# Blocks of 512 and 480 tokens, another form of 1+elu, and six of eight chunk pairs split whole

## The chip, the cores and the metric

The kernel runs on one core of a Trainium2 chip. The metric is the device time of one execution in microseconds. The engines are called PE (TensorE, matrix products; PEld is its weight load), DVE (VectorE), ACT (ScalarE), POOL (GpSimd) and SP (SyncE, which issues the transfers). Each works through its own instructions in order and waits at semaphores for the others. Matrix products write to PSUM, eight banks of 512 float32 values per partition; everything else lies in SBUF.

## The reference

Two stages, cut to what matters:

```
# x: 4 batches of 12480 tokens of 128 channels; inducing: 32 rows
def mab(q, kv):
    s = scale * (q @ kv.T);  a = softmax(s);  return a @ kv
h = mab(inducing, x)              # 32 rows per batch
y = mab(x, h)                     # 4 x 12480 rows of 128
g = elu(y @ w_in)                 # 49920 x 2048
out = g @ w_out                   # 49920 x 128
```

The kernel folds `h @ w_in` into one matrix `hw` of 32 rows per batch, so that layer one of the feed-forward is softmax(x h^T) times `hw`.

## The kernel before

**Blocks and pairs.** The tokens of a batch come in 26 blocks of T = 480, all four batches in 104 blocks. For each block the 2048 hidden channels are sixteen chunks of 128, taken as eight pairs (`cp` 0 to 7). A unit `n` is one pair of one block; there are 832. Tokens are the columns throughout: a pair is a tile of 128 partitions and 2 x 480 columns.

**One unit.** `ffn_in` (L518) does layer one: two matmuls (L523) of a chunk of `hw` against the block's `stk` tile, which holds the softmax weights of the block as stacked high and low parts, in the format fp32r. Result: `ph`, two banks of PSUM; the pool `ps_h` has three such tiles. ACT then writes `e` = exp(ph) (L531). `ffn_mid` (L534) makes elu: for seven of eight pairs ACT clamps the exponential with a Relu (L538) and DVE takes the maximum with `ph` (L539); for the pair with the letter D in `CLAMP` DVE does both (L543, L546). With that `ph` is free. `ffn_split` (L548) copies the first of the two chunks to fp32r as `gh` (DVE, L552; in fp32r a part of 12 bits is exact), and POOL makes the rest `gl` (L555). `ffn_out` (L557) is layer two (L575): the chunk that isn't split goes as one float32 matmul (`e` against `wo_n`), the split one as three fp32r matmuls (`gh` against `wo_h` and `wo_l`, `gl` against `wo_h`). They accumulate in `po`, one bank; after the eighth pair DVE transposes it (L582) and SP stores it.

**Order.** PE runs in the written order: layer one of unit n, then layer two of unit n - LAG, with LAG = 6. The other engines get their order from a planner ahead of time. `e` lies in EB = 7 buffers, `gh` and `gl` in GB = 4 each; a buffer that is still to be read makes the writer wait.

**Attention.** For a batch's first stage and for the softmax of the second, groups of four blocks are worked on beside the feed-forward: scores by PE (L273, L449), exponentials by ACT, transposes and sums by DVE, the subtraction and the normalising by POOL (L466, L479), gathering by PE (L347). `attend_stack` (L483) splits the weights into `ahi` and `alo`; SP copies them into the `stk` tiles, four pieces of 32 rows for a block. `stack_h` builds `hw` in the same way. `attend` and `first_half` hold the places of these steps, counted in blocks, in tables. The last batch has no such work beside its later blocks.

**Start.** `first_batch` loads batch 0 and the weights, which come as float64 pairs of words and are taken apart by `Weight` on DVE, ACT and POOL; then the feed-forward begins. The first block goes alone.

```
for n, (b, k, cp) in enumerate(units):
    ffn_in(n)
    while done <= n - min(LAG, RAMP + n // 4):
        ffn_out(done)
        done += 1
    if n >= 1:
        ffn_mid(n - 1)
        ffn_split(n - 1)
    while side and side[0][0] <= n / NCP:
        side.pop(0)[1]()
```

Of the kernel before, what the change touches and what calls it, by code (L numbers as in the profile page):

```python
# [17 lines left out]
P = 128  # L18
Q = 32
T = 480  # L20
U = T // Q
# [9 lines left out]
def kernel(  # L31
# [12 lines left out]
    assert C == P and M == Q and N % T == 0 and F % 256 == 0  # L44
    NBLK = N // T
    GROUPS = [(g, min(4, NBLK - g)) for g in range(0, NBLK, 4)]
    NG = len(GROUPS)
    NH = (NBLK + 1) // 2
# [3 lines left out]
    assert len(SPLIT) == NCP  # L52
    CHUNKS_S = [2 * cp + i for cp in range(NCP) for i in range(SPLIT[cp] + MORE[cp])]
    CHUNKS_N = [f for f in range(NFC) if f % 2 >= SPLIT[f // 2]]
# [16 lines left out]
    xtp = ctx.enter_context(tc.tile_pool(name="xtp", bufs=NH + 2))  # L71
# [15 lines left out]
    # Two banks of PSUM take turns for a block's output; the one at rest serves the attention.  # L87
# [33 lines left out]
    # The feed-forward's weights come as float64: sign, 11 bits of exponent, 52 of mantissa. They  # L121
    # are read as pairs of 32-bit words and rounded to float32 here.
# [10 lines left out]
    class Weight:  # L133
        """A slice of float64 weights on its way to float32."""

        def __init__(self, raw):
            self.raw = raw.rearrange("p (f two) -> p f two", two=2)

        def take_apart(self):
            lo, hi = self.raw[:, :, 0], self.raw[:, :, 1]  # L140
            part = [
                stk.tile([P, WS], U32, tag="stk", name=f"w_{n}")
                for n in ("exp", "scale", "low", "top")
            ]
            e, scale, low, top = part
            nc.vector.tensor_scalar(
                out=e, in0=hi, scalar1=20, scalar2=0x7FF,
                op0=ALU.logical_shift_right, op1=ALU.bitwise_and,
            )
            nc.scalar.activation(e.bitcast(F32), e, AF.Relu, bias=rebias)  # L150
            nc.scalar.activation(
                e.bitcast(F32), e.bitcast(F32), AF.Relu, bias=largest, scale=-1.0
            )
            nc.gpsimd.tensor_scalar(
                out=scale, in0=e.bitcast(F32), scalar1=-254.0, scalar2=-float(1 << 23),
                op0=ALU.add, op1=ALU.mult,
            )
            nc.vector.tensor_scalar(
                out=top, in0=hi, scalar1=0xFFFFF, scalar2=0x100000,
                op0=ALU.bitwise_and, op1=ALU.bitwise_or,  # L160
            )
            nc.scalar.activation(low.bitcast(F32), lo, AF.Copy, scale=2.0**-52)
            nc.scalar.activation(e.bitcast(F32), hi.bitcast(I32), AF.Sign)
            self.scale, self.low, self.top = scale.bitcast(F32), low.bitcast(F32), top
            self.sign = e.bitcast(F32)
# [50 lines left out]
    def load_xT(b, h):  # L216
        n = min(2, NBLK - 2 * h) * T
        xq = xqp.tile([P, 2 * U, Q], F32, tag="xq", name=f"xq_{b}_{h}")
        src = x[b, 2 * h * T : 2 * h * T + n, :]
        for dq in range(4):  # L220
            nc.sync.dma_start(
                xq[dq * Q : (dq + 1) * Q, : n // Q, :],
                src[:, dq * Q : (dq + 1) * Q].rearrange("(u t) d -> t u d", t=Q),
            )
        t = xtp.tile([P, 2 * T], F32, tag="xT", name=f"xT_{b}_{h}")
        tc.keep_in_program_order(
            nc.vector.transpose(t[:, :n], xq.rearrange("p u d -> p (u d)")[:, :n])  # L227
        )
        xT[b, h] = t

    def transpose_first(b, g):
        """x^T of a group out of its tokens on the partitions."""
        g0, nq = GROUPS[g]
        np_ = nq * Q
        halves = []
        for h in range(g0 // 2, (g0 + nq + 1) // 2):
            xT[b, h] = xtp.tile([P, 2 * T], F32, tag="xT", name=f"xT_{b}_{h}")
            halves.append(xT[b, h].rearrange("p (j t u) -> p j t u", j=2, u=U))
        for v in range(0, U, UP):
            n = min(UP, U - v)  # L240
# [26 lines left out]
    def scores(b, g):  # L267
        g0, nq = GROUPS[g]
# [11 lines left out]
        # Within a block, token t * U + u goes to column (u, t).  # L280
# [10 lines left out]
    # The softmax over the tokens goes in two phases of groups: the first takes the maximum of its  # L291
    # own groups, the second that of all, and scales what the first has summed.
# [48 lines left out]
    def gather(b, g):  # L341
        st = state[b]
        np_ = GROUPS[g][1] * Q
# [74 lines left out]
    def stack_h(b):  # L418
        # Rows: high, low, high, low; against them the rows of a are high, high, low, low.
# [3 lines left out]
        for c in range(4):  # L423
            for i in range(4):
# [3 lines left out]
                )  # L428
        st["hw"] = hw

# [1 line left out]
    # The very first block goes alone, its rows four times from the start.  # L432
    stacks = {}

    def blocks_of(b, g):
        g0, nq = GROUPS[max(g, 0)]
# [34 lines left out]
    def attend_norm(b, g):  # L471
        s = state[b]["s2", g]
        np_ = s.shape[0]
# [9 lines left out]
    def attend_stack(b, g):  # L483
        s = state[b]["s2", g].rearrange("p u m -> p (u m)")
        np_ = s.shape[0]
        aT = once.tile([P, T], F32, tag="aT", name=f"aT_{b}_{g}")[:np_]
        nc.vector.transpose(aT, s)  # L487
        if lone(b, g):
            t = op.tile([P, T], F32R, tag="o", name=f"stk_{b}_{g}")
            nc.scalar.copy(t, aT)  # L490
            low = t[2 * Q :]
            nc.vector.tensor_sub(low, aT[2 * Q :], low.bitcast(F32))
            stacks[b, 0] = t
# [267 lines left out]
```

## Time and profile before

| | |
|---|---|
| median of 3 runs | 1813.05 us (1812.02 to 1813.22) |
| profiled execution: span from the first to the last instruction | 1811.1 us; no other time of this execution is given |
| busy share of the span | PE 95%, DVE 92%, ACT 87%, POOL 66% |
| mean granted clock of TensorE | 0.992 |
| instructions | 25049 |

How to read the rows. A row of the groups has the line, the engine, the operation, the tile written and those read, the shapes and the count; behind the first bar the busy time in us and the mean of one in ns; behind the second bar the engine's idle time just before, and what ended most of it. A row of the timeline has the start, the duration, the engine and line, the tiles, and in brackets the idle time before it with what ended it; `x2` means several merged instructions. A row of the waits has the engine and line that waited, the one it waited for, the total in us, the times and the longest. A row of the windows has the stretch, its length, busy time and count of the instructions asked for, the granted clock and the DMA share and rate. A matmul's recorded end is modelled, and consecutive ones overlap in the records; distances between starts are surer. A plain float32 matmul shows as two records.

### The profile page before, as it was taken

How to read it: one execution, taken by the hardware profiler on the slowest of the kernel's cores; microseconds unless marked ns; L12 is line 12 of the kernel's file. 1: busy time of each engine (PE TensorE's matmuls, PEld its weight loads, DVE VectorE, ACT ScalarE, POOL GpSimd, SP SyncE). 2: the span in 40 equal slices, each digit the busy share in tenths (PEclk: the TensorE clock that was granted, in tenths of full speed). 3: DMA queues.
4: the chain of work that ended last, by engine and by line, in shares of the span. 5: the costliest groups of instructions: out<-in, count | busy, mean ns of one | idle time of the engine just before them, and what ended most of it. 6: DMA issues, size and time to landing. Idle time of an engine off the chain costs nothing.

```text
span 1811.1 us, 25049 instructions
## 1 busy us (share of the span) xinstructions
PE 1728.0 (95%) x7268; PEld 1139.2 (63%) x7268; DVE 1669.4 (92%) x2308; ACT 1570.9 (87%) x1804; POOL 1196.6 (66%) x1007
## 2 busy tenths in 40 slices
PE   7699999999999999999999999999999999999998
PEld 5356666666666666666665666666666666666665
DVE  6999899998899988999899999899899999999998
ACT  6888888889888888889898888888888988888886
POOL 3866666666766666666666666666667667777776
PEclk9799999999999999999999999999999999999999
DMA  6555232222245423222225343222122211111111
GB/s 236 113 85 93 47 72 61 52 51 48 58 69 93 74 55 72 39 60 45 53 53 94 57 80 66 45 55 44 22 54 42 39 33 23 35 31 22 28 16 18
DMA packets 391574, 105.67 MB, mean 58 GB/s; under 512 B 367216, under 2 KB 382480, under 8 KB 391184
## 3 DMA queue, kind: packets, MB, share of 16 engines
q1 hardware_dynamic: 391440, 104.08, 29.5%
q8 instruction: 60, 0.98, 0.2%
q14 instruction: 74, 0.61, 0.1%
HBM read 48.94 MB, written 25.56 MB: 41 GB/s over the span
## 4 chain that ended last, share of the span: by engine, by line
PE 76%; DVE 15%; issue 5%; ACT 2%; DMA 1%; POOL 1%; SPq 0%; DVEq 0%; ACTq 0%; POOLq 0%
PE po L575 53%; PE ph L523 18%; DVE e L539 4%; DVE gh L552 4%; DVE e L546 2%; PE ps_hh L347 1%; DVE xT L227 1%; PE ps_s L273 1%; PE ps_t L449 1%; ACT e L531 1%; DVE e L543 1%; DMA xq<-in_x_dram 1%; ACT e L538 1%; PE ps_x L244 1%; DVE aT L487 0%
## 5 line engine op out<-in xcount | busy, mean ns | idle before, releaser
L555 POOL TENSOR_TENSOR gl<-e,gh 128x480 fp32r<-128x480 f32 x850 | 1064.4, 1254 | 537.5 <-DVE gh L552 359.7
L531 ACT ACTIVATE e<-ph 128x960 f32<-128x960 f32 x832 | 798.6, 961 | 173.1 <-PE ph L523 151.3
L539 DVE SCALAR_TENSOR_TENSOR e<-e,ph 128x960 f32<-128x960 f32 x728 | 827.1, 1139 | 67.9 <-ACT e L538 63.6
L575 PE MATMUL po<-e,wo_n 128*128 128x480 f32 x1628 | 789.0, 566 | 0.2 <-DVE s L457 0.2
L538 ACT ACTIVATE e<-e 128x960 f32<-128x960 f32 x728 | 729.5, 1005 | 20.1
L575 PE MATMUL po<-gh,wo_h 128*128 128x480 f32 x850 | 629.8, 741 | 0.0
L523 PE MATMUL ph<-stk,hw 128*128 128x480 f32 x1648 | 508.9, 390 | 48.8 <-DVE e L546 25.4
L552 DVE CAST gh<-e 128x480 fp32r<-128x480 f32 x850 | 490.8, 579 | 35.0 <-issue 21.1
L523 PEld LDWEIGHTS ph<-stk,hw 128*128 128x128 f32 x1648 | 294.9, 188 | 169.8 <-PE po L575 67.4
L575 PEld LDWEIGHTS po<-e,wo_n 128*128 128x128 f32 x1628 | 306.8, 189 | 48.9 <-PE ph L523 0.6
L575 PE MATMUL po<-gh,wo_l 128*128 128x480 f32 x850 | 322.1, 379 | 0.0
L575 PE MATMUL po<-gl,wo_h 128*128 128x480 f32 x850 | 320.4, 380 | 0.0
L575 PEld LDWEIGHTS po<-gh,wo_l 128*128 128x128 f32 x850 | 161.0, 189 | 175.1 <-issue 174.1
L575 PEld LDWEIGHTS po<-gh,wo_h 128*128 128x128 f32 x850 | 160.4, 189 | 175.8 <-issue 174.1
L575 PEld LDWEIGHTS po<-gl,wo_h 128*128 128x128 f32 x850 | 159.7, 188 | 26.9 <-POOL gl L555 0.6
L546 DVE TENSOR_TENSOR e<-e,ph 128x960 f32<-128x960 f32 x104 | 118.7, 1141 | 0.9
L543 DVE TENSOR_SCALAR e<-e 128x960 f32<-128x960 f32 x104 | 72.9, 701 | 5.4 <-ACT e L531 5.4
L582 DVE STREAM_TRANSPOSE o<-po 128x480 f32<-128x480 f32 x104 | 69.6, 669 | 3.7 <-PE po L575 3.7
L466 POOL TENSOR_TENSOR s<-s,mx 128x480 f32<-128x480 f32 (+2 forms) x28 | 29.6, 1056 | 28.2 <-DVE mx L465 28.2
L227 DVE STREAM_TRANSPOSE xT<-xq 128x960 f32<-128x960 f32 x39 | 45.3, 1162 | 0.0
L498 POOL TENSOR_TENSOR alo<-aT,ahi 128x480 fp32r<-128x480 f32 (+2 forms) x28 | 36.2, 1293 | 6.0 <-ACT ahi L497 5.7
L347 PE MATMUL ps_hh<-xm,e 128*32 128x128 f32 (+1 forms) x840 | 32.4, 291 | 3.6 <-DVE h L356 1.2
(93 smaller groups left out, 530.1 us busy)
## 6 DMA issues: line engine op xcount, KB each, us to landing
out_dram<-o SPq DMA_DIRECT2D x416, 60.0 KB, 1.9
xq<-in_x_dram SPq DMA_DIRECT2D x156, 120.0 KB, 3.6
stk<-ahi SPq DMA_DIRECT2D x206, 60.0 KB, 2.0
stk<-alo SPq DMA_DIRECT2D x206, 60.0 KB, 2.0
xm<-in_x_dram SPq DMA_DIRECT2D x24, 512.0 KB, 4.5
xm<-in_x_dram SPq DMA_DIRECT2D x24, 448.0 KB, 3.7
w_raw<-in_moe_w_in_dram SPq DMA_DIRECT2D x2, 1024.0 KB, 9.0
w_raw<-in_moe_w_out_dram SPq DMA_DIRECT2D x4, 512.0 KB, 4.9
```

The lines of the kernel that those rows point to most:

```text
L227: nc.vector.transpose(t[:, :n], xq.rearrange("p u d -> p (u d)")[:, :n])
L347: nc.tensor.matmul(ps[c * Q : (c + 1) * Q, :C], st["e", g][:np_, u * Q : (u + 1) * Q], st["xm", g, u - u % UP][:np_, u % UP, :], start=(u ...
L523: nc.tensor.matmul(ph[:, i, :T], state[b]["hw"][:, f * P : (f + 1) * P], stacks[b, k], start=True, stop=True,)
L531: nc.scalar.activation(e, ph[:, :, :T], AF.Exp)
L538: nc.scalar.activation(e, e, AF.Relu, bias=1.0, scale=-1.0)
L539: nc.vector.scalar_tensor_tensor(out=e, in0=e, scalar=-1.0, in1=ph[:, :, :T], op0=ALU.mult, op1=ALU.max)
L543: nc.vector.tensor_scalar(out=e, in0=e, scalar1=1.0, scalar2=-1.0, op0=ALU.min, op1=ALU.add)
L546: nc.vector.tensor_tensor(out=e, in0=e, in1=ph[:, :, :T], op=ALU.max)
L552: nc.vector.tensor_copy(gh[i], e[:, i, :])
L555: nc.gpsimd.tensor_sub(gl[i], e[:, i, :], gh[i].bitcast(F32))
L575: nc.tensor.matmul(po[:, :T], w, g, start=(cp == 0 and i == 0), stop=(cp == NCP - 1 and i == len(parts) - 1),)
L582: nc.vector.transpose(o.rearrange("p u d -> p (u d)"), po[:, :T])
```

## The change

Tokens: a batch is now 25 blocks, 15 of 512 and 10 of 480, in seven groups (`GROUPING`), so 100 blocks and 800 units. Elu: a row of ones in `hw` against a constant row block of 1/32 in `stk` makes layer one give H = 1 + h, and the tile is then g = 1 + elu = min(exp(H - 1), max(H, 1)): ACT writes exp with a bias of -1, one DVE instruction does the rest for every pair. The pieces in `stk` and `hw` become three of 32 rows and a constant fourth.

Splitting: each pair has a letter. P (places 0, 3, 5): both chunks are split; ACT writes `gh` = g - 1 to fp32r, POOL takes 1 off `e` in place and subtracts `gh`. D (places 1, 4, 7): both chunks are split; DVE writes g over `ph` in PSUM, ACT writes `gh` from there, and DVE makes `gl` = (g - 1) - gh from `ph`. N (places 2, 6): neither is split; POOL takes 1 off `e`, and layer two has two float32 matmuls. In the last batch from block 8 on, place 6 is a D. `gh` and `gl` are now tiles of the whole pair.

Buffers: `e` has 5 (was 7), `gh` 4 and `gl` 3 (of double width), `stk` six fixed tiles (was 8), `xm` 2 (was 3), LAG is 5 (was 6). `ph` stays at 3. `first_batch` puts the tokens of batch 0 into the buffers of `xm`, `e`, `gh` and `gl`, and the weights are taken apart in place.

```diff
-T = 480
-SPLIT = [1, 1, 1, 1, 1, 1, 1, 1]
-MORE = [0, 0, 1, 0, 0, 0, 0, 0]
-CLAMP = "AAADAAAA"
+TM = 512
+GROUPING = [(4, 512), (4, 512), (4, 512), (3, 512), (4, 480), (4, 480), (2, 480)]
+PLAN = "PDNPDPND"
+PLAN_CALM = "PDNPDPDD"
...
-    LAG = 6
+    LAG = 5
-    EB = 7
-    GB = 4
+    EB = 5
+    GHB = 4
+    GLB = 3
-    XB = 3
+    XB = 2
+    STK = 6
...
     def stack_h(b):
         for c in range(4):
-            for i in range(4):
+            for i in range(3):
                 nc.sync.dma_start(
...
+        nc.gpsimd.memset(hw[3 * Q :, :].bitcast(F32), 1.0)
...
+    homes = []
+    for i in range(STK):
+        homes.append(stk.tile([P, TM], F32R, tag=f"stk{i}", name=f"stk{i}"))
+        nc.gpsimd.memset(homes[i][3 * Q :, :].bitcast(F32), 1.0 / Q)
+
+    def home(b, k):
+        T = BLOCKS[k][1]
+        stacks[b, k] = homes[(b * NBLK + k) % STK][:, :T]
+        return stacks[b, k]
...
         for j, k in enumerate(blocks_of(b, g)):
-            t = stk.tile([P, T], F32R, tag="stk", name=f"stk_{b}_{k}")
-            for c in range(4):
+            t = home(b, k)
+            for c in range(3):
...
         e = gp.tile([P, 2, T], F32, tag="e", name=f"e_{n}")
-        nc.scalar.activation(e, ph[:, :, :T], AF.Exp)
+        nc.scalar.activation(e, ph, AF.Exp, bias=-1.0)
...
     def ffn_mid(n):
-        if CLAMP[cp] == "A":
-            nc.scalar.activation(e, e, AF.Relu, bias=1.0, scale=-1.0)
-            nc.vector.scalar_tensor_tensor(
-                out=e, in0=e, scalar=-1.0, in1=ph[:, :, :T], op0=ALU.mult, op1=ALU.max
-            )
-        else:
-            ...
+        v = live[n]
+        v["g"] = v["ph"] if plan(n) == "D" else v["e"]
+        nc.vector.scalar_tensor_tensor(
+            out=v["g"], in0=v["ph"], scalar=1.0, in1=v["e"], op0=ALU.max, op1=ALU.min
+        )
+
     def ffn_split(n):
-        for i in range(split(n)):
-            gh.append(ghp.tile([P, T], F32R, tag="gh", name=f"gh_{n}_{i}"))
-            nc.vector.tensor_copy(gh[i], e[:, i, :])
-        for i in range(split(n)):
-            gl.append(glp.tile([P, T], F32R, tag="gl", name=f"gl_{n}_{i}"))
-            nc.gpsimd.tensor_sub(gl[i], e[:, i, :], gh[i].bitcast(F32))
+        v, how = live[n], plan(n)
+        shape = list(v["e"].shape)
+        if how != "N":
+            v["gh"] = ghp.tile(shape, F32R, tag="gh", name=f"gh_{n}")
+            nc.scalar.activation(v["gh"], v["g"], AF.Copy, bias=-1.0)
+        if how == "D":
+            v["gl"] = glp.tile(shape, F32R, tag="gl", name=f"gl_{n}")
+            nc.vector.scalar_tensor_tensor(
+                out=v["gl"], in0=v["g"], scalar=-1.0, in1=v["gh"].bitcast(F32),
+                op0=ALU.add, op1=ALU.subtract,
+            )
+        else:
+            nc.gpsimd.tensor_scalar(
+                out=v["e"], in0=v["e"], scalar1=-1.0, scalar2=1.0, op0=ALU.add, op1=ALU.mult
+            )
+        if how == "P":
+            v["gl"] = glp.tile(shape, F32R, tag="gl", name=f"gl_{n}")
+            nc.gpsimd.tensor_sub(v["gl"], v["e"], v["gh"].bitcast(F32))
...
     def attend(b, g):
-        first = {0: (0.0, 0.13), 1: (1.39, 0.35), 2: (2.3, 0.7)}
-        later = {0: (-2.58, 0.19), 1: (0.07, 0.38)}
-        at, gap = (later if b else first).get(g, (4 * g - 6.7, 0.92))
+        first = {0: (0.0, 0.13), 1: (1.39, 0.35)}
+        later = {0: (-2.58, 0.19), 1: (0.9, 0.38)}
+        at, gap = (later if b else first).get(g, (GROUPS[max(g, 0)][0] - 4.7, 0.92))
...
-        room = [(xmp, "xm")] * XB + [(gp, "e")] * EB
-        spare = [(xqp, "xq")] * 2 + [(xtp, "xT")] * 2
+        room = [(xmp, "xm")] * XB + [(gp, "e")] * EB + [(ghp, "gh")] * GHB + [(glp, "gl")] * GLB
```

More of the change, by code (lines that the diff above doesn't have):

```diff
@@ L43 @@
     F = w_in.shape[1] // 2
-    assert C == P and M == Q and N % T == 0 and F % 256 == 0
-    NBLK = N // T
-    GROUPS = [(g, min(4, NBLK - g)) for g in range(0, NBLK, 4)]
+    assert C == P and M == Q and F % 256 == 0
+    assert N == sum(n * t for n, t in GROUPING)
+    GROUPS, BLOCKS, HALVES = [], [], []
+    for n, t in GROUPING:
+        GROUPS.append((len(BLOCKS), n, t))
+        for j in range(0, n, 2):
+            HALVES.append((len(BLOCKS) + j, min(2, n - j), len(GROUPS) - 1))
+        for _ in range(n):
+            BLOCKS.append((sum(u for _, u in BLOCKS), t))
+    NBLK = len(BLOCKS)
     NG = len(GROUPS)
-    NH = (NBLK + 1) // 2
+    NH = len(HALVES)
+    HALF_OF = {k: (h, k - k0) for h, (k0, n, _) in enumerate(HALVES) for k in range(k0, k0 + n)}
     UP = 8
@@ L488, in attend_stack @@
         if lone(b, g):
[L489 to L493, printed above, removed]
+            t = home(b, 0)
+            nc.scalar.copy(t[: 3 * Q], aT[: 3 * Q])
+            low = t[2 * Q : 3 * Q]
+            nc.vector.tensor_sub(low, aT[2 * Q : 3 * Q], low.bitcast(F32))
             return
@@ L506, in attend_stack, with plan @@
                 )
-            stacks[b, k] = t
     outs = {}
     live = {}
-    def split(n):
+    def plan(n):
         b, k, cp = units[n]
-        return SPLIT[cp] + (MORE[cp] if b == B - 1 and k >= CALM else 0)
+        return (PLAN_CALM if b == B - 1 and k >= CALM else PLAN)[cp]
     def ffn_in(n):
         b, k, cp = units[n]
-        ph = ps_h.tile([P, 2, 512], F32, tag="ph", name=f"ph_{n}")
+        T = BLOCKS[k][1]
+        ph = ps_h.tile([P, 2, 512], F32, tag="ph", name=f"ph_{n}")[:, :, :T]
         for i in range(2):
@@ L565, in ffn_out @@
             f = 2 * cp + i
-            if i >= split(n):
-                parts.append((0, wo_n[:, WHERE_N[f], :], e[:, i, :]))
+            if how == "N":
+                parts.append((0, wo_n[:, WHERE_N[f], :], v["e"][:, i]))
             else:
                 w = WHERE_S[f]
-                parts.append((1, wo_h[:, w, :], gh[i]))
-                parts.append((1, wo_l[:, w, :], gh[i]))
-                parts.append((2, wo_h[:, w, :], gl[i]))
+                parts.append((1, wo_h[:, w, :], v["gh"][:, i]))
+                parts.append((1, wo_l[:, w, :], v["gh"][:, i]))
+                parts.append((2, wo_h[:, w, :], v["gl"][:, i]))
         parts.sort(key=lambda v: v[0])
@@ L582, in ffn_out @@
             nc.vector.transpose(o.rearrange("p u d -> p (u d)"), po[:, :T])
[L583 removed]
+            at = b * N + BLOCKS[k][0]
+            dst = out[at : at + T, :]
             for dq in range(4):
@@ L602, in first_half @@
         for g in range(NG):
-            for h in range(2 * g, min(2 * g + 2, NH)):
-                room = (
-                    attend(b - 1, (h - 2) // 2)[0][0] - (b - 1) * NBLK + 0.3 if h > 1 else 0.0
-                )
+            for h in [h for h in range(NH) if HALVES[h][2] == g]:
+                room = attend(b - 1, HALVES[h - 1][2])[0][0] - (b - 1) * NBLK + 0.3 if h else 0.0
                 at = max(at + 0.5, room)
@@ L621, in first_half @@
                 steps.append((at + 1.19, lambda g=g: gather(b, g)))
-                for j, v in enumerate(range(0, U, UP)):
+                for j, v in enumerate(range(0, GROUPS[g][2] // Q, UP)):
                     steps.append((at - 0.7 + 0.1 * j, lambda g=g, v=v: load_xm(b, g, v)))
@@ L643, in first_batch @@
         for g, v in PIECES:
-            if v and g > NG - 5:
-                load_xm(b, g, v, *spare.pop())
-            else:
-                load_xm(b, g, v, *room.pop(0))
+            load_xm(b, g, v, *room.pop(0))
         win += load_w_in(1)
```

128 lines of the change are left out of this document (65 added, 63 removed).

## The prediction

> **What bounds the kernel now.** I read the page first (busy shares, the chain that ended last, the costliest groups), then the windows, then the timeline of single instructions.
>
> ```profile
> span 1811.1 us, 25049 instructions
> PE 1728.0 (95%) x7268; PEld 1139.2 (63%) x7268; DVE 1669.4 (92%) x2308; ACT 1570.9 (87%) x1804; POOL 1196.6 (66%) x1007
> PE 76%; DVE 15%; issue 5%; ACT 2%; DMA 1%; POOL 1%; SPq 0%; DVEq 0%; ACTq 0%; POOLq 0%
> L555 POOL TENSOR_TENSOR gl<-e,gh 128x480 fp32r<-128x480 f32 x850 | 1064.4, 1254 | 537.5 <-DVE gh L552 359.7
> L531 ACT ACTIVATE e<-ph 128x960 f32<-128x960 f32 x832 | 798.6, 961 | 173.1 <-PE ph L523 151.3
> L539 DVE SCALAR_TENSOR_TENSOR e<-e,ph 128x960 f32<-128x960 f32 x728 | 827.1, 1139 | 67.9 <-ACT e L538 63.6
> L538 ACT ACTIVATE e<-e 128x960 f32<-128x960 f32 x728 | 729.5, 1005 | 20.1
> L552 DVE CAST gh<-e 128x480 fp32r<-128x480 f32 x850 | 490.8, 579 | 35.0 <-issue 21.1
> ```
>
> TensorE (PE) is the bound, VectorE (DVE) is close behind. A busy PE isn't yet PE at full rate, so I price its passes by distances between starts:
>
> ```profile
> 61.47 1.17 PE L523 MATMUL ph<-stk_-1_833,hw 128*128 128x480 f32 x2 [11.43 <-DMA hw<-hw_h]
> ...
> 89.95 1.01 PE L449 MATMUL ps_t<-xT,hT 128*32 128x480 f32 x8
> 90.89 0.70 PE L523 MATMUL ph<-stk,hw 128*128 128x480 f32 x2
> ...
> 604.44 1.07 PE L347 MATMUL ps_hh<-xm,e 128*32 128x128 f32 x30
> 605.44 0.70 PE L523 MATMUL ph<-stk,hw 128*128 128x480 f32 x2
> ...
> 613.11 0.60 PE L523 MATMUL ph<-stk,hw 128*128 128x480 f32 x2
> 615.01 0.60 PE L523 MATMUL ph<-stk,hw 128*128 128x480 f32 x2
> ...
> 1797.06 0.38 PE L575 MATMUL po<-gl,wo_h 128*128 128x480 f32 x1
> 1798.14 0.60 PE L575 MATMUL po<-gl,wo_h 128*128 128x480 f32 x2
> 1800.04 0.97 PE L575 MATMUL po<-e,wo_n 128*128 128x480 f32 x2
> 1801.50 0.97 PE L575 MATMUL po<-e,wo_n 128*128 128x480 f32 x2
> 1805.65 0.38 PE L575 MATMUL po<-gl,wo_h 128*128 128x480 f32 x1
> ```
>
> Five fp32r passes lie between 1797.06 and 1798.14: 0.217 us a pass. Layer two of a pair takes 1801.50 - 1800.04 = 1.46; less three passes, the plain f32 matmul (two records) costs 0.81. An undisturbed pair takes 1.90 (613.11 to 615.01), which is five passes and 0.81. All 832 pairs: 1577 us, less 3 for the 18 extra splits at the end: 1574. The attention's matmuls cost 0.94 for four blocks (89.95 to 90.89) of either score kind and 1.0 for a gathering group: over the feed-forward's stretch 7 x 6.1 + 21 x 1.0 + some 3 = 67 us. That stretch runs from 61.5 to 1805.9, 1744 us, so PE loses about 103, 0.9 us a block besides a slow ramp. The windows, grouped on the exponential (L531: busy, count), agree: 191 pairs in 400 us are 2.09 a pair with attention, 153 in 310 are 2.03 without.
>
> ```profile
> 100.00:500.00 400.00, 182.83 (x191) 1.00 0.33 62
> 1480.00:1790.00 310.00, 145.85 (x153) 1.00 0.15 26
> ...
> PE ph L523 <- DVE e L546: 25.4, 40, 1.6
> PE ph L523 <- DVE e L539: 22.6, 33, 1.6
> ```
>
> The two rows of the waits show what late work looks like: layer one has no free `ph` until DVE has read an old one. `ph` has three buffers; the change keeps three.
>
> **The change, part by part.** *PE.* A split pair (P or D) takes 2 + 6 passes, 1.736; a plain one (N) two passes and two f32 matmuls, 2.054. A block of six and two: 14.52 against 8 x 1.895 = 15.16, at 480 tokens. No row shows an fp32r pass of 512 columns: between 0.217 (cost by instruction) and 0.231 (by column). I take 0.231, since 2 x 0.94 for eight column-tiled calls and the 0.81 give no sign of a large fixed part; a block of 512 is then 15.49. Sum: 60 x 15.49 + 40 x 14.52 - 5 (17 pairs that become D at the end) = 1505, so -69; at the other end 1447, so -127.
>
> *DVE and ACT.* Per 480-token block L539 and L552 alone are 1317.9 / 104 = 12.7 us, and the pair clamped on DVE adds two instructions. Afterwards: 8 + 3 instructions like L539, 11 x 1.139 = 12.5. ACT had 15 passes over a pair per block, and will have 14. I price `gh` as L531 where it reads PSUM (D) and L538 where it reads SBUF (P). So neither is a new bound by sum. A write of DVE into PSUM (`g` of a D pair) has no row; I put it at L539's 1.139, with 0.1 us either way (it may also gain). Longer blocks:
>
> ```profile
> L582 DVE STREAM_TRANSPOSE o<-po 128x480 f32<-128x480 f32 x104 | 69.6, 669 | 3.7 <-PE po L575 3.7
> L227 DVE STREAM_TRANSPOSE xT<-xq 128x960 f32<-128x960 f32 x39 | 45.3, 1162 | 0.0
> L497 ACT CAST ahi<-aT 128x480 fp32r<-128x480 f32 x23 | 13.5, 588 | 7.5 <-DVE aT L487 7.1
> L154 POOL TENSOR_SCALAR w_scale<-w_exp 128x256 uint32<-128x256 f32 x16 | 7.2, 447 | 20.5 <-ACT w_exp L151 19.4
> L204 POOL TENSOR_TENSOR wo_l<-wo,wo_h 128x128 fp32r<-128x128 f32 x9 | 4.7, 521 | 0.4
> ```
>
> From 480 to 960 columns DVE grows by 1.03 ns a column and ACT (588 to L538's 1005) by 0.87. Over 64 more columns the pair's operations become 1.205 (DVE), 1.02 (exp, `gh`).
>
> *POOL.* The difference goes from 128 (521) to 480 columns (1254): 2.08 ns a column, 2.39 for a pair of 1024, three a block. The new e - 1, five a block, has only L154 near it: between 0.45 (all fixed) and 1.79 (all by column); I take 1.1. With (1196.6 - 1064.4) / 104 = 1.3 for the rest that makes 5.5 + 7.2 + 1.3 = 14.0 us per 512 block, 17.4 at the upper end. Its result is needed five pairs after layer one (about 10 us); exp, mid, `gh`, e - 1 and difference take 1.0 + 1.2 + 1.0 + 1.1 + 2.4 = 6.7. Two or three us of queue are covered; beyond that PE waits at `gl`. The Trainium skill, "GPSIMD Engine Reference", section 4.1, says that two-input elementwise work is about half of VectorE's speed there and one-input work roughly at line rate. The trace agrees on the first (1254 ns for 480 columns against L539's 1139 for 960); by the second e - 1 would be near ACT's 1.0, and the block 13.5, an estimate.
>
> *The chain of a D pair: the term that decides.* Today `ph` is free after exp, clamp and one DVE pass. For P and N it will be free after exp and mid, about 2.5 us. For D it stays in use through exp, mid, `gh`, and `gl`. The hand-overs:
>
> ```profile
> 640.07 1.01 ACT L538 ACTIVATE e<-e 128x960 f32<-128x960 f32 x1
> 641.11 1.16 DVE L539 SCALAR_TENSOR_TENSOR e<-e,ph 128x960 f32<-128x960 f32 x1 [0.42 <-ACT e L538]
> ...
> 653.52 1.01 ACT L538 ACTIVATE e<-e 128x960 f32<-128x960 f32 x1
> 654.44 0.95 ACT L531 ACTIVATE e<-ph 128x960 f32<-128x960 f32 x1
> ...
> 1788.84 0.60 PE L523 MATMUL ph<-stk,hw 128*128 128x480 f32 x2
> 1789.28 0.97 PE L575 MATMUL po<-e,wo_n 128*128 128x480 f32 x2
> 1789.54 0.97 ACT L531 ACTIVATE e<-ph 128x960 f32<-128x960 f32 x1 [0.93 <-PE ph L523]
> ...
> 1792.11 1.14 DVE L546 TENSOR_TENSOR e<-e,ph 128x960 f32<-128x960 f32 x1
> 1793.39 0.67 PE L523 MATMUL ph<-stk,hw 128*128 128x480 f32 x2 [0.61 <-DVE e L546]
> ```
>
> PE to ACT 0.26 after the last pass is in (1789.28 to 1789.54), ACT to DVE 0.03, DVE to PE 0.14; DVE to ACT, unseen, 0.1 (0.03 to 0.14). At 512: 0.26 + 1.02 + 0.03 + 1.205 + 0.1 + 1.02 + 0.03 + 1.205 + 0.14 = 5.01. PE comes back for that buffer three pairs on, after three layer twos and two layer ones: 5.43 us with an N among them, 5.09 without. So the D at place 1 has 0.4 to spare, that at 4 has 0.1, if nothing queues ahead of them. The D at place 7 has not: `e` has five buffers, so its exp writes where pair 2 (an N) lies, which layer two reads as it is, and which PE does only after layer one of pair 7. Its chain starts 2 x 0.864 = 1.73 late: 6.74 against 5.43, PE stands 1.3 us per block (1.29 at 480). The D at place 4 is hit by the same thing once removed: exp of pair 3 waits for layer two of the N at 6 of the block before, holds ACT 0.93 (653.52 to 654.44 shows the spacing) and then DVE; it would start its own exp 0.46 + 0.26 = 0.72 after that layer two and starts at 0.26 + 0.93 = 1.19, then waits 0.2 for pair 3's mid: 0.6 late after its 0.1 of slack. How much is paid hangs on the order that the planner gives ACT and DVE; between 0 and 0.6 I take 0.3.
>
> In these windows (six of eight pairs) PE would have stood, so three quarters of the attention's 0.72 us a block cost nothing there. A block of 512 with attention: 15.49 + 0.72 + 1.6 - 0.54 = 17.27; of 480: 14.52 + 0.68 + 1.6 - 0.51 = 16.29; without attention (the last 17 blocks) 17.09 and 16.12. Sum over 60 and 40 blocks: 53 x 17.27 + 30 x 16.29 + 7 x 17.09 + 10 x 16.12 = 1685.
>
> The Trainium skill, "PSUM — Partial Sum Buffer", summary of rules, says to evacuate PSUM promptly because it is tight. That speaks against D pairs: by this rule (mid writes to SBUF) the stalls would go and the sum would be the first rival's; nothing in the trace of before holds `ph` so long, so no run here shows it yet.
>
> *The rest.* Start: 12 instead of 16 transfers build `hw`; if the 11.43 us wait shrinks in proportion, 2.9, else 0; I take -2.5. The weights' decoding has the same instructions in other buffers: 0, within 2 us. The memset of `hw`'s last rows on POOL lies two blocks ahead of its use in POOL's idle third; if that cover went, at most 2048 x 2.08 ns = 4.3 us a batch. The stack takes 297 transfers where it took 412, so SP's queue is shorter, off the path. Six `stk` homes instead of eight: the copy for a group is due about when the old block is done, two blocks (34 us) before use; cover gone, it costs a transfer's 2 us, seldom.
>
> Before the stretch 61.5 - 2.5, ramp 9.5 as now (eight pairs from 61.5 to 81), after it 5.2: 1685 + 59 + 9.5 + 5.2 = 1759 against the span of 1811.1. The runs' median lies 2 us above that span. Some queueing like today's 0.9 a block remains where slack is 0.1 to 0.4; I put 10 us for it: 1770.
>
> **The rivals.** *PE stays the bound* (the stalls hide): 1505 + 67 + 93 (today's losses) + 59 + 9.5 + 5.2 + 2 = 1741; with cheap 512 passes 1683. For it: DVE and ACT have less to do. Against it: 6.74 over 5.43.
>
> *The copy waits behind an exponential* (slower). When `gh` of the D at 7 is ready, the exp two pairs on is ready too: after pair 2's layer two, 0.46 + 1.38 + 0.46 + 0.26 = 2.56 for the exp, 0.26 + 1.02 + 0.03 + 1.205 + 0.1 = 2.62 for `gh`. If ACT takes the exp first, the chain grows by 0.93, each block: 1770 + 93 = 1863. It decides from 0.4 a block on (1811 - 1770 over 100), about every second block: 1817. For it: ACT is busy 87% and will be nearly so; the order is planned ahead, not chosen at run time. Against it: the same planner sees this wait.
>
> *POOL binds*: e - 1 at 1.79 makes 17.4 us a block of 512 and 16.4 of 480, about the forecast's own blocks, so it needs queueing on top: 1700 to 1800 whichever way, part of the others' ranges.
>
> *Nothing to tell*: gains and stalls cancel within 0.2%, about what a measurement of this kernel can tell.
>
> **How the numbers follow.** Forecast, D chains pay 1.3 to 1.9 a block (1750 to 1805): 0.38. PE-bound (1690 to 1750): 0.24. Copy behind the exponential or more (1817 to 1870): 0.30. No difference: 0.08. So faster 0.62, same 0.08, slower 0.30. The range leaves out the cheap-pass end and the worst queueing: 1718 to 1855; the forecast's own is 1750 to 1805.
>
> **What would show it.** Right: PE waits at layer one for DVE `gl` lines, mostly for one pair in eight, 1 us and more each; ACT waits for PE's plain matmuls before exp; 17 us between output transposes of 512-blocks; DVE's share falls below 87%. Wrong: exp never waits for layer two (then 1741), `gl` of P pairs reaches PE late (POOL), an fp32r pass of 512 columns at 0.217, or `gh` starting a whole exp after its mid (slower).

## The result, and the profile after

The changed kernel takes 1761.66 us (median of four runs, 1761.6 to 1763.55) against 1813.13 us of the kernel before on the same chip (1812.02 to 1813.63): a ratio of 0.972, with a 95% interval of 0.9706 to 0.9734. Its profiled execution has a span of 1759.5 us, 51.6 less than before. One changed letter in a table of the new kernel brings it to 1728.5 us (experiment `k1_calm_as_rest`).

The page of the changed kernel, its busy shares, the chain that ended last, and three groups:

```profile
span 1759.5 us, 22797 instructions
PE 1659.5 (94%) x7480; PEld 1177.4 (67%) x7480; DVE 1551.8 (88%) x1635; ACT 1425.0 (81%) x1662; POOL 1331.7 (76%) x955
PE 73%; DVE 12%; ACT 5%; issue 3%; POOL 3%; DMA 3%; SPq 0%; DVEq 0%; ACTq 0%; POOLq 0%
L568 ACT ACTIVATE e<-ph 128x1024 f32<-128x1024 f32 (+1 forms) x800 | 803.5, 1005 | 241.3 <-PE ph L560 237.9
L560 PE MATMUL ph<-stk,hw 128*128 128x512 f32 (+1 forms) x1600 | 563.0, 433 | 60.7 <-DVE gl L586 43.7
L586 DVE SCALAR_TENSOR_TENSOR gl<-ph,gh 128x1024 fp32r<-128x1024 f32 (+1 forms) x317 | 375.8, 1185 | 40.4 <-PE po L618 25.9
```

TensorE is still the bound, and VectorE has gone from 92% to 88%. ACT's exponential waits for layer one and, unlike what the prediction had, never for layer two. Two idle entries belong together and turn out to be the point of this case: layer one (L560) waits for `gl` of a D pair, and `gl` itself waits for layer two (`po`).

How far each kernel gets, by windows grouped on the exponential (stretch, length, ACT busy and count of the exponentials, clock, DMA share and rate), before and after:

```profile
100.00:1300.00 1200.00, 548.62 (x572) 1.00 0.32 61
1430.00:1700.00 270.00, 126.65 (x132) 1.00 0.16 29
```

```profile
100.00:1300.00 1200.00, 573.52 (x571) 1.00 0.31 59
1300.00:1430.00 130.00, 68.58 (x68) 1.00 0.19 35
1430.00:1700.00 270.00, 126.05 (x126) 0.99 0.15 25
```

Beside the attention the pairs come as fast as before (571 against 572 in 1200 us), but each now carries 499.2 tokens on average instead of 480: 1200 / 571 x 8 = 16.81 us a block, 3.7% less per token. Near the end, where nothing runs beside the feed-forward and where six of eight pairs became seven, a pair takes 270 / 126 = 2.14 us against 2.05 before. In the 130 us ahead of it a pair took 1.91, 15.3 us a block against 17.1, although those blocks are longer. The gain is made in the first four fifths, and some of it is lost in the last.

The third place is the start. TensorE's rows before and after:

```profile
48.97 1.06 PE L405 MATMUL ps_hw<-win_sb,hT 128*32 128x512 f32 x8
61.47 0.77 PE L523 MATMUL ph<-stk_-1_833,hw 128*128 128x480 f32 x1 [11.43 <-DMA hw<-hw_h]
```

```profile
57.26 1.94 PE L427 MATMUL ps_hw<-win_sb,hT 128*32 128x512 f32 x8
68.54 0.79 PE L560 MATMUL ph<-stk,hw 128*128 128x512 f32 x1 [9.35 <-DVE stk L528]
```

The feed-forward begins 7.1 us later. The wait in front of it became shorter (9.35 against 11.43); the product that makes `hw` comes 8.3 later.

**Where the last stretch loses.** The timeline of one block near the end, cut to what belongs to the D pair at place 6 (the row 1610.37 holds the middle parts of places 6 and 7):

```profile
1609.31 1.14 DVE L586 SCALAR_TENSOR_TENSOR gl<-ph,gh 128x960 fp32r<-128x960 f32 x1
...
1610.37 2.22 DVE L574 SCALAR_TENSOR_TENSOR ph<-ph,e 128x960 f32<-128x960 f32 x2
...
1611.56 0.97 ACT L583 ACTIVATE gh<-ph 128x960 fp32r<-128x960 f32 x1 [0.17 <-DVE ph L574]
...
1611.69 2.25 POOL L596 TENSOR_TENSOR gl<-e,gh 128x960 fp32r<-128x960 f32 x1
...
1613.06 0.60 PE L618 MATMUL po<-gl,wo_h 128*128 128x480 f32 x2
...
1613.80 1.16 DVE L586 SCALAR_TENSOR_TENSOR gl<-ph,gh 128x960 fp32r<-128x960 f32 x1 [1.21 <-PE po L618]
...
1615.01 0.70 PE L560 MATMUL ph<-stk,hw 128*128 128x480 f32 x2 [1.35 <-DVE gl L586]
```

`gh` is ready at 1612.53, but `gl` is not begun before 1613.80, after the two matmuls of 1613.06 have read an older `gl`. Only three `gl` exist: the D at 4 has just filled one (1609.31), POOL is filling one for the P at 5 (1611.69), and the third still holds the P at 3 until its layer two. TensorE does that layer two, has next a layer one whose `ph` the D at 6 still holds, and stands: 1.35 us of recorded idle time for the write of `gl` and the hand-overs (from 1613.06 to 1615.01 pass 1.95 us, where two passes take 0.43). It is a ring: layer one of pair n + 3 waits for `gl` of n, that waits for layer two of n - 3, and this stands just ahead of the same layer one in TensorE's order. The addresses that the planner gave the tiles (they stand in the built program, not in the traces) agree: in these 17 blocks the split pairs at places 6, 7, 0 and 1 take the `gl` of the unit three back once the fourth D has come, and everywhere else a split pair takes one four back, because an N lies between and uses none.

### The profile page after: what moved, and what is told of

The parts are those of the page before. It is cut to its first block, busy times and chain, and to the rows that moved or that the text cites. A ratio compares the mean times of both kernels' runs of the same rounds, so it can differ in the third digit from the quotient of the medians.

```text
span 1759.5 us, 22797 instructions
## 1 busy us (share of the span) xinstructions
PE 1659.5 (94%) x7480; PEld 1177.4 (67%) x7480; DVE 1551.8 (88%) x1635; ACT 1425.0 (81%) x1662; POOL 1331.7 (76%) x955
## 4 chain that ended last, share of the span: by engine, by line
PE 73%; DVE 12%; ACT 5%; issue 3%; POOL 3%; DMA 3%; SPq 0%; DVEq 0%; ACTq 0%; POOLq 0%
PE po L618 51%; PE ph L560 18%; DVE gl L586 4%; ACT e L568 3%; DVE ph L574 2%; DVE e L574 2%; DVE xT L241 2%; ACT gh L583 1%; PE ps_hh L369 1%; PE ps_t L485 1%; PE ps_s L293 1%; POOL gl L596 1%; DMA w_raw<-in_moe_w_in_dram 1%; DMA xq<-in_x_dram 1%; DMA xm<-in_x_dram 1%
## 5 line engine op out<-in xcount | busy, mean ns | idle before, releaser
L568 ACT ACTIVATE e<-ph 128x1024 f32<-128x1024 f32 (+1 forms) x800 | 803.5, 1005 | 241.3 <-PE ph L560 237.9
L591 POOL TENSOR_SCALAR e<-e 128x1024 f32<-128x1024 f32 (+1 forms) x483 | 495.4, 1031 | 354.2 <-ACT gh L583 309.0
L596 POOL TENSOR_TENSOR gl<-e,gh 128x1024 fp32r<-128x1024 f32 (+1 forms) x300 | 704.4, 2348 | 19.8 <-PE po L618 0.9
L574 DVE SCALAR_TENSOR_TENSOR e<-ph,e 128x1024 f32<-128x1024 f32 (+1 forms) x483 | 571.5, 1187 | 75.1 <-ACT e L568 73.1
L560 PE MATMUL ph<-stk,hw 128*128 128x512 f32 (+1 forms) x1600 | 563.0, 433 | 60.7 <-DVE gl L586 43.7
L618 PE MATMUL po<-gh,wo_h 128*128 128x512 f32 (+1 forms) x1234 | 481.7, 390 | 10.5 <-ACT e L568 6.5
L618 PE MATMUL po<-gh,wo_l 128*128 128x512 f32 (+1 forms) x1234 | 478.9, 388 | 0.0
L560 PEld LDWEIGHTS ph<-stk,hw 128*128 128x128 f32 x1600 | 289.9, 189 | 247.1 <-issue 92.8
L574 DVE SCALAR_TENSOR_TENSOR ph<-ph,e 128x1024 f32<-128x1024 f32 (+1 forms) x317 | 378.3, 1196 | 47.7 <-ACT e L568 46.4
L586 DVE SCALAR_TENSOR_TENSOR gl<-ph,gh 128x1024 fp32r<-128x1024 f32 (+1 forms) x317 | 375.8, 1185 | 40.4 <-PE po L618 25.9
L618 PE MATMUL po<-gl,wo_h 128*128 128x512 f32 (+1 forms) x1234 | 379.1, 388 | 2.8 <-POOL gl L596 2.8
```

The lines of the kernel that those rows point to most:

```text
L560: nc.tensor.matmul(ph[:, i], state[b]["hw"][:, f * P : (f + 1) * P], stacks[b, k], start=True, stop=True,)
L568: nc.scalar.activation(e, ph, AF.Exp, bias=-1.0)
L574: nc.vector.scalar_tensor_tensor(out=v["g"], in0=v["ph"], scalar=1.0, in1=v["e"], op0=ALU.max, op1=ALU.min)
L586: nc.vector.scalar_tensor_tensor(out=v["gl"], in0=v["g"], scalar=-1.0, in1=v["gh"].bitcast(F32), op0=ALU.add, op1=ALU.subtract,)
L591: nc.gpsimd.tensor_scalar(out=v["e"], in0=v["e"], scalar1=-1.0, scalar2=1.0, op0=ALU.add, op1=ALU.mult)
L596: nc.gpsimd.tensor_sub(v["gl"], v["e"], v["gh"].bitcast(F32))
```

## The experiments

Each was run in three rounds or more against the kernel before; a sum in us is the difference of medians.

**k1_calm_as_rest.** The end in the order of the rest.

```diff
-PLAN_CALM = "PDNPDPDD"
+PLAN_CALM = "PDNPDPND"
```

> The last 17 blocks get the plan of the others (an N at place 6 instead of a D). Theory (neighbouring D pairs keep two of three ph buffers): in the changed kernel this stretch takes 149 pairs in 320 us, 17.2 us a block, where PE needs about 14.5 to 15.5; with the usual plan it should lose some 0.5 a block as elsewhere: 36 us less, about 1726. Rival (the end is slow whatever the plan): PE has 0.3 us more a block, +5, 1767. The wait of layer one for gl should nearly vanish after 1430 us by the theory.

1728.51 us, ratio 0.9537 (0.9523 to 0.9551): 33.1 less than the changed kernel, near the expected 1726, and the fastest of all. The windows of all engines in the last stretch (PE, PEld, DVE, ACT, POOL busy and counts, clock, DMA), changed kernel and then this one:

```profile
1430.00:1700.00 270.00, 246.18 (x995) 180.74 (x993) 232.58 (x227) 221.92 (x243) 190.76 (x125) 0.99 0.15 25
```

```profile
1430.00:1700.00 270.00, 270.00 (x1090) 200.09 (x1089) 243.50 (x238) 230.42 (x257) 225.94 (x155) 1.00 0.16 27
```

TensorE has 0.3 us more to do per block and is never seen idle. So the loss at the end hangs on this one letter. That it comes from neighbouring D pairs, as expected, is another matter: see k7 and k10.

**k2_e_in_turn, k8_ph_in_turn, k3_e_ph_in_turn.** Buffers in a fixed rotation, for `e`, for `ph`, and for both, everything else as in the changed kernel (end included).

```diff
-        e = gp.tile([P, 2, T], F32, tag="e", name=f"e_{n}")
+        e = gp.tile([P, 2, T], F32, tag=f"e{n % EB}", name=f"e_{n}")
...
-        ph = ps_h.tile([P, 2, 512], F32, tag="ph", name=f"ph_{n}")[:, :, :T]
+        ph = ps_h.tile([P, 2, 512], F32, tag=f"ph{n % 3}", name=f"ph_{n}")[:, :, :T]
```

> e's five buffers are handed out strictly in turn, as the prediction assumed. In the changed kernel they are not: the D at place 7 always takes the buffer of the D at place 4, free since its mid. Theory (the arithmetic was right, only the turn was assumed): exp of place 7 waits for layer two of the N five pairs before, 1.3 us a block less what the freely chosen ph buffers still hide: 1790 to 1890, and ACT's exp shows waits for PE's plain matmuls. Rival (the wait would have been hidden anyway): 1762.

> ph alone in turn, e free. By the prediction's sum, without the wait for e, the D at 4 has 0.1 and those at 1 and 7 have 0.4 us to spare, so little would be lost: 1770 to 1820. Rival, from k3's 2233 against k2's 1817: the turn of ph is what costs, because the sum left out what stands ahead of a D's four steps in the queues of ACT and DVE (one operation each, about 1 us): then 1950 or more.

> Both e (five) and ph (three) strictly in turn: the prediction's model entire. By its sum a block of 512 with attention takes 17.3 us or more, against about 16.6 in the changed kernel, and both D chains at 4 and 7 pay: theory 1830 to 1880, slower than with e in turn alone. Rival (turns do not matter): 1762.

1816.98 (1.0024; 1.0015 to 1.0034), 1986.96 (1.0964; 1.0946 to 1.0983) and 2233.16 (1.2321; 1.2287 to 1.2355): 55, 225 and 471 us more than the changed kernel. The first lies in its theory's range, the second went the rival's way (1950 or more), and the third is far above all that was expected of it. The waits, of `e` in turn and then of `ph` in turn:

```profile
ACT e L568 <- PE po L618: 179.3, 153, 2.9
PE ph L560 <- DVE gl L586: 49.8, 67, 3.3
```

```profile
PE ph L560 <- DVE gl L586: 194.8, 203, 3.8
POOL gl L596 <- PE po L618: 65.2, 29, 4.1
```

With `e` in turn the exponential waits for layer two, as the prediction had it for the changed kernel; there this wait does not occur at all. With `ph` still chosen freely it costs 0.55 us a block, not 1.3. With `ph` in turn the loss is four times as large. Its timeline, around one D pair:

```profile
1716.29 1.23 DVE L574 SCALAR_TENSOR_TENSOR ph<-ph,e 128x1024 f32<-128x1024 f32 x1 [0.81 <-ACT e L568]
...
1718.70 0.73 PE L560 MATMUL ph<-stk,hw 128*128 128x512 f32 x2 [2.19 <-DVE gl L586]
...
1719.46 1.02 ACT L568 ACTIVATE e<-ph 128x1024 f32<-128x1024 f32 x1 [2.26 <-PE ph L560]
...
1720.43 1.03 ACT L583 ACTIVATE gh<-ph 128x1024 fp32r<-128x1024 f32 x1
```

The middle part is done at 1717.52, and `gh` begins 2.9 us later: ACT stands 2.26 at an exponential whose layer one waits for another pair's `gl`, and `gh` is queued behind it. That is the prediction's slower rival, at work in a kernel that lacks the free choice of `ph`. The Trainium skill, "PSUM — Partial Sum Buffer", summary of rules, asks to evacuate PSUM promptly; `k8_ph_in_turn` agrees that holding it can be very dear (225 us). But k1 holds the tiles of its D pairs in the same way and has no recorded idle time of TensorE at the end: what decides is who is made to wait for them.

**k4_all480.** Blocks of 480 throughout, 26 a batch, with the rest of the change.

```diff
-GROUPING = [(4, 512), (4, 512), (4, 512), (3, 512), (4, 480), (4, 480), (2, 480)]
+GROUPING = [(4, 480), (4, 480), (4, 480), (4, 480), (4, 480), (4, 480), (2, 480)]
```

> All blocks of 480 (104 of them), the rest as changed. Theory (a pass costs by column: 0.23 at 512, 0.2165 at 480): PE has 5 us more, and four more blocks' worth of transposes and hand-overs, 1765 to 1775. Rival (512 columns come nearly free): PE has 60 us more, about 1820. A second rival: the longer blocks cost by their longer chains, then 1750.

1768.06 us (0.9758; 0.9743 to 0.9772): 6.4 more than the changed kernel, as its theory had it; the changed kernel's fp32r passes of 512 columns start 0.23 apart (next section). The longer block is worth little by itself; the gain comes from the other parts.

**k5_four_split, k7_seven_split.** Four or seven of eight pairs split, in every block.

```diff
-PLAN = "PDNPDPND"
-PLAN_CALM = "PDNPDPDD"
+PLAN = "PDNNPNND"        # k5, both tables; k7: "PDNPDPPD"
+PLAN_CALM = "PDNNPNND"
```

> Four pairs split whole and four plain (plan PDNNPNND throughout), everything else as changed: PE has the same number of passes per column as before the change, 15.16 us a block of 480. Beside k1, 1728.5, which has six split: theory (PE binds, each pair that goes from plain to split gives its 0.32 us to the time) 1728 + 2 x 0.33 x 100 = about 1794, so that 18 of the 84 us that k1 gained over before come from elsewhere. Rival (the splitting work of DVE, ACT and POOL costs as much as it brings): 1730 to 1750.

> Seven pairs split whole (place 6 is a P instead of an N, throughout). PE has 0.33 us less a block: 1696 beside k1's 1728.5 if PE still binds. Theory: POOL gets a fourth difference and has 4 x (1.05 + 2.4) + 1.05 + 1.3 = 16.2 us a block of 512 against PE's 15.1 + 0.7, so POOL binds and its queue delays gl: 1720 to 1790, with PE waiting for gl of POOL. Rival (POOL's queue is hidden): 1696.

1779.26 (0.9818; 0.9804 to 0.9833) and 1769.78 (0.9766; 0.9751 to 0.9781), 51 and 41 above k1, which has six. The first lies between its theory (1794) and its rival (1750), the second in its theory's range. k5 gives TensorE the same passes for the tokens as the kernel before and is 33 us faster than it: that part is less standing. Whether it comes from the shorter elu or from the blocks, buffers and order that changed with it, no run separates. The step from four to six split pairs is worth the other 51, or 0.25 us a pair of the 0.318 at 480 columns (2.054 - 1.736) by which a split pair is shorter. The step to seven is a loss: POOL is now near its limit, as this row of k7's page shows, and seven split pairs stand in a row.

```profile
PE 1650.5 (93%) x7646; PEld 1199.2 (68%) x7646; DVE 1539.7 (87%) x1618; ACT 1507.4 (85%) x1743; POOL 1582.1 (90%) x1072
```

k7 also tells what the ring of `gl` does alone. By the addresses its `gl` go round as at the end of the changed kernel (places 6, 7, 0 and 1 take the one three back), but place 6 is a P. TensorE's wait at layer one for `gl` in the last stretch (1430 to 1700), in the changed kernel and then in k7:

```profile
PE ph L560 <- DVE gl L586: 23.7, 25, 3.1
```

```profile
PE ph L560 <- DVE gl L586: 2.8, 7, 0.8
```

The last 17 blocks, from their first exponential to the end of the kernel, take 302.8 us in the changed kernel, 276.6 in k7 and 268.1 in k1. So the full ring alone costs little there. It is dear where the pair that waits for its `gl` is a D and holds a `ph` meanwhile, with another D beside it.

**k6_op3.** k1 with a third buffer for `op`, to see what holds the start.

```diff
-    op = ctx.enter_context(tc.tile_pool(name="op", bufs=2))
+    op = ctx.enter_context(tc.tile_pool(name="op", bufs=3))
```

> k1 with three buffers instead of two for the output tiles, which the change also uses for the parts of the weights at the start. The changed kernel's feed-forward began at 68.5 us where the old one began at 61.5, and the prediction had 59. Theory (the decoding of the weights waits for these two buffers): the start moves back by up to 7 us, 1721 to 1726. Rival (the order of the start is what costs): 1728, as k1.

1728.78 us (0.954; 0.9526 to 0.9554), k1's time, as the rival had it; the first layer one comes at 68.44. The theory that these two buffers hold the start falls.

**k9_calm_four_p.** Seven split pairs at the end, as in the changed kernel, but the seventh a P at place 2 instead of a D at place 6.

```diff
-PLAN_CALM = "PDNPDPDD"
+PLAN_CALM = "PDPPDPND"
```

> k1, but in the last 17 blocks, where no attention runs, place 2 is a P instead of an N: as many splits there as the changed kernel has, without neighbouring Ds. Theory (neighbours were the trouble; POOL needs 14.9 us a block of 512 and 13.9 of 480 there, PE 15.2 and 14.2): it keeps the 0.32 us a block that the seventh split saves PE, 1721 to 1726. Rival (a seventh split costs more than it brings wherever it runs, as in k7, where it cost 41 us over 100 blocks): 1732 to 1740.

1741.07 us (0.9607; 0.9591 to 0.9623), 12.6 above k1 and 20.6 below the changed kernel, just above its rival's range and far from its theory's. In the waits of the last stretch (1430 to 1700) TensorE's two rows are now POOL's, and `gl` waits for layer two as it does in the changed kernel, on both engines that write it:

```profile
PEld po L618 <- POOL gl L596: 16.9, 19, 3.1
PE po L618 <- POOL gl L596: 9.3, 11, 2.7
DVE gl L586 <- PE po L618: 8.3, 7, 2.1
POOL gl L596 <- PE po L618: 7.9, 10, 1.6
```

A seventh split pair costs more than it saves, in either form. Both ends have seven split pairs in a row, across the border of two blocks (places 7 and 0 to 5 here, 3 to 7, 0 and 1 in the changed kernel), but the fourth P costs 12.6 and the fourth D 33.

**k10_d_beside_d, k11_n_spread.** k1's counts (three P, three D, two N) in other orders, in every block.

```diff
-PLAN = "PDNPDPND"
+PLAN = "PDDPNPND"        # k10, both tables; k11: "PDNPDNPD"
```

> The same three P, three D and two N as k1, for all blocks, in another order (PDDPNPND): the D pairs at 1 and 2 are neighbours. No instruction more or less than k1. Theory (it is neighbouring D pairs that hold two of the three ph buffers, as at the end of the changed kernel, where it cost 2.1 us a block): 1 to 2 us a block, 1830 to 1930, PE waiting at layer one for gl. Rival (the end of the changed kernel was slow for its fourth D, that is for more work on DVE, not for the neighbours): 1728.

> k1 with places 5 and 6 exchanged (PDNPDNPD): each D but the last has an N behind it, and the P pairs, POOL's work, come every third pair. The same instructions. k1 still loses some 0.7 us a block over PE's passes. Theory (part of that is POOL's two P pairs two places apart): 1710 to 1725. Rival (an N ahead of a P beside a D shortens what PE has to do while the last D holds ph: 1.38 instead of 1.73): 1730 to 1750.

1772.23 (0.9776; 0.9762 to 0.9791) and 1754.98 (0.9682; 0.9667 to 0.9696): 44 and 26 us above k1 with the same work. Both expectations missed: k10 is far from its theory (1830 and more) and from its rival (1728), k11 above both of its ranges. In k10 two D are neighbours: 0.44 us a block, where the fourth D at the end of the changed kernel costs 33 us in 17 blocks, or 1.9. In k11 no two D are, but four split pairs follow one another. The wait of `gl` for layer two, in the 1200 us from 100 to 1300, in k1 (three in a row) and in k11:

```profile
DVE gl L586 <- PE po L618: 8.9, 11, 1.5
```

```profile
DVE gl L586 <- PE po L618: 36.2, 39, 1.6
```

**k12_high_by_dve.** k1 with `gh` of the P pairs made by VectorE.

```diff
-            nc.scalar.activation(v["gh"], v["g"], AF.Copy, bias=-1.0)
+            if how == "P":
+                nc.vector.tensor_scalar(
+                    out=v["gh"], in0=v["g"], scalar1=-1.0, scalar2=1.0, op0=ALU.add, op1=ALU.mult
+                )
+            else:
+                nc.scalar.activation(v["gh"], v["g"], AF.Copy, bias=-1.0)
```

> The order of k1 (the end in the order of the rest), with the high part of the P pairs made by VectorE in place of ScalarE. The theory (with PE always busy in k1, what matters is which engine comes late, and VectorE has some 11% of its time left): three more passes a block on VectorE at 0.75 us (one input and one output, scaled from the 410 ns of its 480-column passes) to 1.2 us each are 2.3 to 3.6 us a block where about 1.9 us were free, so VectorE becomes the bound: 1760 to 1830. The rival (the chain of a P pair no longer waits for ScalarE between its middle part and its difference, and VectorE has the room): 1720 to 1730.

1832.27 us (1.0111; 1.0094 to 1.0128), 104 above k1 and just beyond the theory's upper end. The page's busy shares, and the groups kept apart by shape:

```profile
PE 1694.5 (93%) x7446; PEld 1172.6 (64%) x7446; DVE 1741.9 (95%) x1918; ACT 1166.3 (64%) x1343; POOL 1368.8 (75%) x970
L584 DVE TENSOR_SCALAR gh<-e 128x1024 fp32r<-128x1024 f32 x180 | 140.3, 780 | 0.2
```

The pass itself is cheap (0.78 us), and VectorE is full: 236 us of such passes (300, of both lengths) were put where k1 had 194 us left over its span, and it is at once the bound. So in this kernel the high part of the P pairs belongs on ScalarE.

## Why the prediction was right, and which steps failed

It said 1770 and faster; 1761.7 came. The sign and most terms held, but the stall that it put into every block is not there, and that the total came so near is in part luck. The span splits like this (prediction of 1759 plus 10 of queueing, against 1759.5): start +9.5; the 83 blocks beside attention, from 68.5 to about 1455 (652 pairs at 1430, 12 more at 2.14), 1386 instead of 1422, or -35; the last 17 blocks and the tail 304 instead of 288, or +17.

The -35 isn't the missing stall. Between 100 and 1300 us a block took 16.81 us where the forecast's two lengths average 16.88 (0.6 x 17.27 + 0.4 x 16.29), with 0.1 of queueing on top. The forecast had put its stall, 1.6 - 0.54 = 1.06 a block net, where the kernel before lost 0.9 a block, and had kept only 10 us of these losses. The stall didn't come, and losses of that size stayed: the first rival, which kept them, has 16.73 by the same average (15.1 for TensorE's passes, 0.7 for the attention, 0.93 of losses). Most of the -35 lies at the ramp and in the first blocks of the last batch, where less runs beside the feed-forward: 15.3 us a block between 1300 and 1430, forecast as 17.3. So the sum of a block was right in size and wrong in what it is made of.

**Right: TensorE's sums.** An undisturbed block of 512, from the timeline:

```profile
705.12 0.62 PE L560 MATMUL ph<-stk,hw 128*128 128x512 f32 x2
705.58 1.88 PE L618 MATMUL po<-e,wo_n 128*128 128x512 f32 x4
...
705.84 1.02 ACT L568 ACTIVATE e<-ph 128x1024 f32<-128x1024 f32 x1
...
708.23 0.39 PE L618 MATMUL po<-gh,wo_h 128*128 128x512 f32 x1
708.45 0.39 PE L618 MATMUL po<-gh,wo_l 128*128 128x512 f32 x1
...
720.75 0.62 PE L560 MATMUL ph<-stk,hw 128*128 128x512 f32 x2
```

From place 3 of one block to place 3 of the next, 705.12 to 720.75, are 15.63 us where 15.49 was worked out; passes start 0.22 to 0.23 apart, two of layer one 0.46 (705.12 to 705.58): the price by column, 0.231, and not 0.217.

**Right: the prices of the new operations.** Groups kept apart by shape:

```profile
L591 POOL TENSOR_SCALAR e<-e 128x1024 f32<-128x1024 f32 x293 | 306.7, 1052 | 205.5 <-ACT gh L583 180.5 <-DVE e L574 22.1
L596 POOL TENSOR_TENSOR gl<-e,gh 128x1024 fp32r<-128x1024 f32 x180 | 432.8, 2405 | 11.3 <-PE po L618 0.9
L574 DVE SCALAR_TENSOR_TENSOR e<-ph,e 128x960 f32<-128x960 f32 x190 | 217.4, 1147 | 32.4 <-ACT e L568 31.2
L574 DVE SCALAR_TENSOR_TENSOR ph<-ph,e 128x960 f32<-128x960 f32 x130 | 150.0, 1158 | 22.2 <-ACT e L568 21.8
```

e - 1 takes 1.05 (1.1 was taken between 0.45 and 1.79), the difference 2.41 (2.39), a write into PSUM 0.01 more than one into SBUF (1.158 against 1.147; 1.139 was taken). The rule of the Trainium skill, "GPSIMD Engine Reference", section 4.1, that one-input work runs about at line rate, made 1.0 of it as an estimate, and the row agrees. POOL does not bind: TensorE waits for its `gl` once, for 2.8 us.

**Failed: "`e` has five buffers, so its exp writes where pair 2 (an N) lies".** This is the step that carried the forecast's 1.3 us a block at place 7 and 0.3 at place 4. The buffers are not handed out in turn. The planner takes one that is free: by the addresses, place 7 takes the `e` of the D at place 4 in all 100 blocks, since a D needs its `e` only up to its middle part. The rows above show it for the pair ahead of the D at place 4: the exponential at 705.84 belongs to the layer one of 705.12, which is place 3, and starts 0.26 after its last pass, beside the layer two of the N at place 6 of the block before (705.58, four records, until 706.89). For place 7 a block near the end shows the same: layer one at 1609.71, then the layer two of the N at place 2, which runs until 1611.37, and the exponential beside it.

```profile
1609.71 0.59 PE L560 MATMUL ph<-stk,hw 128*128 128x480 f32 x2
1610.14 1.77 PE L618 MATMUL po<-e,wo_n 128*128 128x480 f32 x4
1610.42 0.96 ACT L568 ACTIVATE e<-ph 128x960 f32<-128x960 f32 x1
1611.37 0.97 PE L560 MATMUL ph<-stk,hw 128*128 128x480 f32 x2
```

So the sign named there as wrong for the forecast, an exponential that never waits for layer two, is what came. Even in turn the price would have been 0.55 a block while `ph` is free (k2).

**Failed: "PE comes back for that buffer three pairs on".** The same for `ph`: a P's or N's tile is free early and serves again after two units, while the D at 4 keeps its own for four (place 0 takes it in 83 of 100 blocks). The slack of 0.4 and 0.1 that the chain of 5.01 was measured against is a pair larger. What a true turn costs, k8 shows: 2.25 us a block.

**Not seen: the ring of `gl`.** The prediction asked which engine would bind and which `e` and `ph` come free; of `gl` it counted only when it is ready, not the three buffers. It priced the fourth D at the end as a gain of 5 on TensorE (in 1505; the block sum of 1685 has these 17 pairs as N and leaves the 5 out); it cost 33. k1 shows that the D at place 6 is the cause. That the third `gl` is what it runs into is read from the trace and the addresses, and is in line with k9 and k11; a kernel with a fourth `gl` was not run. The ring isn't enough by itself: k7 has the same and loses little by it, and in k10's last stretch no D pair's `gl` waits for layer two although five split pairs follow one another. Two neighbouring D pairs aren't enough either: in k10 the last 17 blocks take 273.7 us, 5.6 more than in k1. The end of the changed kernel has both; how its loss divides between them and VectorE's own order stays open.

**Failed: the start, "I take -2.5".** It is +7.1, because of steps ahead of `hw`'s product, not of the transfers that were costed: the product comes 8.3 later, and from there to layer one it is 1.2 shorter (11.28 against 12.50). The term that failed is the one put at 0 within 2 us. k6 excludes one suspect. k4 is of more use: with blocks of 480 and the same start its first layer one comes at 58.6, as forecast, and yet its second block begins no earlier (first exponential at 91.2 us, against 89.6 in the changed kernel and 81.9 before). So the late first layer one isn't by itself what costs; what holds the first block stays open.

**The rivals.** PE-bound at 1741 is nearest to what the design does: without the fourth D the kernel is at 1728.5, with TensorE 96% busy. The copy does fall behind an exponential in the changed kernel too, here of the D at place 4, whose middle part is done at 710.31:

```profile
709.08 1.23 DVE L574 SCALAR_TENSOR_TENSOR ph<-ph,e 128x1024 f32<-128x1024 f32 x1 [0.55 <-ACT e L568]
...
710.60 1.01 ACT L568 ACTIVATE e<-ph 128x1024 f32<-128x1024 f32 x1
...
711.50 1.02 ACT L583 ACTIVATE gh<-ph 128x1024 fp32r<-128x1024 f32 x1
```

With `ph` chosen freely TensorE seldom pays for it: between 100 and 1300 us it waits at layer one for `gl` twelve times, 14.9 us in all, not once in eight pairs. Only `ph` in turn makes it dear (k8). VectorE's share is 88%, not under 87%.

## What to carry to other kernels

Before pricing a wait for a buffer, find out who hands buffers out: in a fixed turn, count the units back; by free choice, count how many are in use at once and for how long, and do so for every ring, the one written last included. A letter in a plan that shortens the bound engine's work can lengthen the kernel when it removes the unit that used no buffer of a full ring and puts one there that holds a second scarce buffer while it waits (33 us for one letter here). When a total comes out near, compare it by stretches and by terms: here +9.5, -35 and +17 us stood behind a difference of 9, and a stall that didn't come stood in for losses that were left out.

## What the runs showed of the hardware that was not expected

On VectorE a pass with one input and one output over 1024 columns took 780 ns for SBUF to SBUF (k12), against 1213 in the changed kernel with a second input from PSUM (`e` from `ph` and `e`). Writing the result into PSUM cost hardly more than into SBUF, 1158 against 1147 ns at 960 columns.
